# The last 128-column store as two halves of 64 rows on two queues, and the copy of x to the output in seven pieces instead of eight

## The chip, the cores and the metric

The kernel runs on one core of a Trainium2 chip, in one launch. Times are device microseconds of one execution of the program. Three runs of the kernel before took 177.51, 177.76 and 178.34 us; the median is 177.76 us. Beside them one execution was taken by the hardware profiler.

## The reference

What is computed, cut to what matters (`x` is 1 x 2048 x 512, bfloat16 in and out):

```python
xn = layernorm(x)                                   # over the 512 features, no weights
# A: a diagonal linear recurrence over the 2048 rows, with 512 complex states
Bu = einsum("bld,pd->blp", xn, B_bar)               # complex
h[t] = Lam_bar * h[t-1] + Bu[t]
a = 2 * einsum("blp,dp->bld", h, Cmat).real + xn * Dskip
# B: a gated feed-forward layer, F = 1376
b = (silu(xn @ w_gate) * (xn @ w_up)) @ w_down
return x + a + b
```

The output is thus the sum of x itself, a skip term, the recurrence and the feed-forward layer.

## The kernel before

The 2048 rows are 16 tiles of 128 rows; four tiles make a chunk of 512 rows. Each chunk goes through the normalization, the projection to the states (`bproj_chunk`, L384), the recurrence on VectorE (L394 to L426), the gate and up projections (`gateup_chunk`, L459) and the output (`out_chunk`). In the output stage every row tile has its sums collected in PSUM by TensorE: first the feed-forward part (`out_ffn`, L627), then the recurrence part (`out_ssm`, L640). The order on each engine is the order in which the kernel's Python code issues it (the schedule is manual); VectorE work is queued in a backlog and issued in portions between the matmuls.

The output reaches DRAM in two ways. For the first three chunks (rows 0 to 1535) x is copied to the output by DMA from DRAM to DRAM, without passing the on-chip memory (L896, L897): 1536 rows in eight pieces of 192 rows, all issued by SyncE (SP). Later GpSimd (POOL) issues DMAs that add to what stands there: the sums (L650) and the skip terms (L601). For the last chunk x and the skip term are already in `xall` on the chip; VectorE adds the PSUM tile to it (L643), and a plain store writes the finished rows (L647). SP issues the stores of the tiles 12, 13 and 14 as a whole, 128 rows of 512 columns.

The very last row tile, `n == NT - 1`, is cut into two column blocks (`out_blocks`, L606): columns 0 to 383, then 384 to 511. Block 0 is added by VectorE at L643 and stored by the queue of ScalarE (ACT), 128 rows of 384 columns. Meanwhile TensorE works on block 1, of which VectorE has x and the part already summed added beforehand (L646, into `rest`). The last add of the kernel is block 1 at L643; its store, 128 rows of 128 columns (32 KB, 256 bytes a row), is issued by SP at L647. In the profile, DMAs issued by SP are on queue q1, those of ACT on q10.

Each DMA of SP and ACT signals its landing on one of eight semaphores, handed out in turn in program order (DMAHW0 to DMAHW7); POOL's have eight others. At the end of the program (L941) SP waits for all of these semaphores one after the other, the hardware ones in the order 0 to 7, and then all engines meet in a barrier. In the kernel before, block 0 of the last tile signals DMAHW6 and block 1 DMAHW7.

Of the kernel before, what the change touches and what calls it, by code (L numbers as in the profile page):

```python
# [23 lines left out]
def kernel(  # L24
# [17 lines left out]
    nc = tc.nc  # L42
    _, L, D = A_x.shape
# [3 lines left out]
    CW = 512  # L47
    HW = CW // 2
    NT = L // 128
    NCH = L // CW  # L50
# [34 lines left out]
    out_v = out[0].rearrange("(n p) d -> p n d", p=128)  # L85
# [520 lines left out]
    def out_blocks(n):  # L606

        return ((0, 3 * D // 4), (3 * D // 4, D)) if n == NT - 1 else ((0, D),)
# [11 lines left out]
    def out_ffn(n, b=0):  # L620
        c, i = divmod(n, TPC)
        for lo, hi in out_blocks(n)[b:b + 1]:
            opened = c % 2 == 1 and b == 0
            if not opened:
                o_tiles[n, b] = bank((128, hi - lo))
            for fi in range(nfull):
                nc.tensor.matmul(o_tiles[n, b][:, 0:hi - lo], lhsT=gu(c, fi, fi + 1)[:, 0, i * 128:(i + 1) * 128],  # L627
                                 rhs=wd_sb[:, fi, lo:hi], start=(fi == 0 and not opened), stop=False)

    def out_ssm(n):  # L630
        c, i = divmod(n, TPC)
        last = n >= NT - TPC
        res = xall[:, n, :] if last else opool.tile([128, D], BF16, name="res")[:]
        for b, (lo, hi) in enumerate(out_blocks(n)):
            if b:
                out_ffn(n, b)
            o = o_tiles[n, b]
            for part in range(2):
                for q in range(NQ):
                    nc.tensor.matmul(o[:, 0:hi - lo], lhsT=w_tiles[c][:, part, q, i * 128:(i + 1) * 128],  # L640
                                     rhs=CF[:, part, q, lo:hi], start=False, stop=(part == 1 and q == NQ - 1))
            if last:
                V.tensor_tensor(out=res[:, lo:hi], in0=o[:, 0:hi - lo], in1=rest if b else res[:, lo:hi], op=ALU.add)  # L643
                if b == 0 and hi < D:
                    rest = jidx[:, 0:D - hi]
                    V.tensor_tensor(out=rest, in0=o[:, hi:D], in1=res[:, hi:D], op=ALU.add)  # L646
                (nc.sync if hi == D else nc.scalar).dma_start(out=out_v[:, n, lo:hi], in_=res[:, lo:hi])  # L647
            else:
                nc.scalar.copy(out=res[:, lo:hi], in_=o[:])  # L649
                nc.gpsimd.dma_start(out=out_v[:, n, lo:hi], in_=res[:, lo:hi], accum_op=ALU.add)  # L650
# [183 lines left out]
    def out_chunk(c):  # L834

        multiply(0)
        if c == 0:
            need("cf")
            load_rest()
        for n in range(c * TPC, (c + 1) * TPC):  # L840
            out_ffn(n)
            pump(nfull * 0.2163)
        if c % 2 == 0:
            out_rest(c)
            pump(2 * RT * 0.2163)
        need(f"ssm{c}")
        for n in range(c * TPC, (c + 1) * TPC):
            out_ssm(n)
            pump(2 * NQ * 0.2163)
# [9 lines left out]
    def queue_ssm(c):  # L859
        fwd, back = ssm_ops(c)  # L860
        queue(f"ssm{c}", fwd + back)
# [31 lines left out]
    nc.gpsimd.dma_start(out=dsk_bc[:], in_=A_Dskip.partition_broadcast(128))  # L893
    bproj_chunk(2)
    piece = (NCH - 1) * CW // 8
    for a in range(0, (NCH - 1) * CW, piece):  # L896
        nc.sync.dma_start(out=out[0, a:a + piece, :], in_=A_x[0, a:a + piece, :])  # L897
    queue_ssm(2)
    gateup_chunk(2)
    out_chunk(0)  # L900
# [45 lines left out]
```

## Time and profile before

| what | us |
|---|---|
| median of three runs (lowest, highest) | 177.76 (177.51, 178.34) |
| the profiled execution, its own time | 178.26 |
| its span, first to last instruction | 176.3 |
| TensorE busy with matmuls | 172.8 (98%) |
| VectorE, ScalarE, GpSimd busy | 158.9, 102.7, 27.1 |
| granted TensorE clock, share of full | 1.00 |

The span leaves out some 2 us of the execution that lie before the first or behind the last instruction. Times of single instructions below are counted from the span's start. "SPq" and "ACTq" are the issuing side of SyncE and ScalarE: the duration of a row is that of the issue, not of the transfer; "us to landing" runs from the issue's start until the whole transfer has signalled.

### The profile page before, as it was taken

The numbers are of one execution on the slowest core, as the hardware profiler recorded it, in microseconds if no ns is written. First come the engines' busy times: TensorE is split into PE (matmuls) and PEld (weight loads), VectorE is DVE, ScalarE is ACT, GpSimd is POOL, SyncE is SP. The second block draws the span as 40 slices with busy tenths as digits, with TensorE's granted clock in tenths as the row PEclk, the third lists the DMA queues.
The fourth block names the chain that finished last, engine by engine and source line by source line (L and its number), as shares of the span: only waits on it lengthen the run. The fifth ranks groups of instructions, "written<-read, shape, count | busy, mean of one in ns | idle before, by whom it ended". The sixth has DMA issues, their size and how long they took to land.

```text
span 176.3 us, 2456 instructions
## 1 busy us (share of the span) xinstructions
PE 172.8 (98%) x896; PEld 82.3 (47%) x896; DVE 158.9 (90%) x263; ACT 102.7 (58%) x186; POOL 27.1 (15%) x36
## 2 busy tenths in 40 slices
PE   8999999999999999999999999999999999999993
PEld 4444464454444464444444444445444444444542
DVE  2699999999999999899999999999999999689642
ACT  3159879895996689976044462014766662983100
POOL 5073210032000000000302500014100000530800
PEclk9999999999999999999999999999999999999999
DMA  5994979999999600220005830006410000597741
GB/s 169 366 343 63 168 148 209 283 185 307 110 203 264 170 4 0 55 57 0 2 0 109 91 42 0 0 4 67 52 22 0 2 4 0 70 174 113 81 102 60
DMA packets 34027, 18.05 MB, mean 102 GB/s; under 512 B 24512, under 2 KB 32832, under 8 KB 33888
## 3 DMA queue, kind: packets, MB, share of 16 engines
q1 hardware_dynamic: 30128, 14.26, 35.0%
q0 software_dynamic: 3456, 3.28, 14.9%
q10 hardware_dynamic: 432, 0.36, 0.6%
q8 instruction: 7, 0.11, 0.3%
q14 instruction: 4, 0.03, 0.1%
HBM read 8.33 MB, written 5.24 MB: 77 GB/s over the span
## 4 chain that ended last, share of the span: by engine, by line
PE 98%; DVE 0%; issue 0%
PE ps L459 29%; PE ps L627 20%; PE ps L640 16%; PE ps L384 16%; PE ps L503 8%; PE ps L552 3%; PE ps L801 2%; PE ps L700 2%; PE ps L617 2%; PE ps L239 1%; PE ps L244 0%; DVE xall L643 0%; PE ps L275 0%
## 5 line engine op out<-in xcount | busy, mean ns | idle before, releaser
L426 DVE TENSOR_TENSOR_SCAN g<-r_t,car,u 128x512 bf16<-128x512 f32 x24 | 28.8, 1262 | 0.0
L640 PE MATMUL ps<-CF,wt 128*128 128x512 bf16 (+2 forms) x136 | 28.5, 367 | 0.0
L384 PE MATMUL ps<-xnT,BT 128*128 128x512 bf16 x128 | 28.1, 379 | 0.0
L627 PE MATMUL ps<-wd_sb,guT 128*128 128x512 bf16 (+2 forms) x130 | 26.6, 363 | 0.0
L459 PE MATMUL ps<-xnT,wg 128*128 128x512 bf16 x96 | 24.6, 379 | 0.0
L459 PE MATMUL ps<-xnT,wu 128*128 128x512 bf16 x96 | 24.6, 379 | 0.0
L386 ACT CAST u<-ps 128x512 bf16<-128x512 f32 x32 | 18.0, 590 | 5.7 <-PE ps L384 5.2
L486 ACT CAST u<-ps 128x512 bf16<-128x512 f32 x30 | 18.0, 599 | 5.1 <-PE ps L459 5.1
L640 PEld LDWEIGHTS <-wt 128*128 128x128 bf16 x136 | 12.8, 98 | 15.1 <-DVE xall L597 0.4
L384 PEld LDWEIGHTS <-BT 128*128 128x128 bf16 x128 | 12.5, 98 | 14.9
L627 PEld LDWEIGHTS <-guT 128*128 128x128 bf16 x130 | 12.4, 98 | 13.9
L199 POOL TENSOR_TENSOR rstd<-ve,neg_half 128x1 f32<-128x1 f32 (+1 forms) x7 | 7.0, 1003 | 73.0 <-DVE ve L198 73.0
L649 ACT CAST res<-ps 128x512 bf16<-128x512 f32 x12 | 6.9, 583 | 18.6 <-PE ps L640 18.6
L589 ACT ACTIVATE xr<-xall,nb,rstd 128x512 bf16<-128x512 bf16 x16 | 11.8, 804 | 8.6 <-DVE xall L597 5.0
L650 POOL DMA_DIRECT2D out_dram<-res x12 | 10.5, 1042 | 36.0 <-ACT res L649 30.0
L459 PEld LDWEIGHTS <-wu 128*128 128x128 bf16 x96 | 9.4, 98 | 11.3
L485 ACT ACTIVATE guT<-ps 128x512 bf16<-128x512 f32 x20 | 12.0, 600 | 4.0 <-PE ps L459 3.6
L459 PEld LDWEIGHTS <-wg 128*128 128x128 bf16 x96 | 9.4, 98 | 10.6
L212 ACT ACTIVATE xn<-xall,nb,rstd 128x512 bf16<-128x512 bf16 x8 | 6.2, 816 | 8.2 <-DVE nb L202 8.2
L459 PE MATMUL ps<-xnT,w_end 128*128 128x512 bf16 x48 | 10.8, 379 | 0.0
L189 DVE BATCH_NORM_STATS2 stats<-xall 128x6 f32<-128x512 bf16 x16 | 10.8, 676 | 0.0
L394 DVE TENSOR_TENSOR pm<-g,c 128x2048 bf16<-128x2048 bf16 x8 | 9.8, 1221 | 0.1
(129 smaller groups left out, 237.8 us busy)
## 6 DMA issues: line engine op xcount, KB each, us to landing
out_dram<-in_A_x_dram SPq DMA_DIRECT2D x8, 192.0 KB, 3.2
out_dram<-res POOLq DMA_DIRECT2D x12, 128.0 KB, 3.1
out_dram<-xall POOLq DMA_DIRECT2D x3, 512.0 KB, 6.1
wd_sb<-in_B_w_down_dram SPq DMA_DIRECT2D x1, 1280.0 KB, 8.0
wu<-in_B_w_up_dram SPq DMA_DIRECT2D x4, 256.0 KB, 4.4
wg<-in_B_w_gate_dram SPq DMA_DIRECT2D x4, 256.0 KB, 5.1
xall<-in_A_x_dram SPq DMA_DIRECT2D x1, 1024.0 KB, 7.0
xall<-in_A_x_dram SPq DMA_DIRECT2D x1, 512.0 KB, 6.5
```

What stands on the lines that cost most here:

```text
L189: nc.vector.bn_stats(out=stats[:, n, 0, :], in_=xall[:, n, :])
L384: nc.tensor.matmul(ps[:] if c else by_k(ps[:]), lhsT=BT[:, part, k, q * 128:(q + 1) * 128], rhs=xnT[:, c, k, :] if c else xnT0[:, k], star ...
L386: nc.scalar.copy(out=u_tiles[c][:, part, q, :], in_=ps[:])
L426: V.tensor_tensor_scan(out=g()[:, part, q, :], data0=r_t[:, q:q + 1].to_broadcast([128, CW]), data1=u_tiles[c][:, part, q, :], initial=ini ...
L459: nc.tensor.matmul(ps[:fs, lo:hi], lhsT=wslice(groups, fi, k), rhs=xnT[:, c, k, lo:hi], start=(k == 0), stop=(k == KD - 1))
L485: nc.scalar.activation(out=gu(c, fi, fi + 1)[:fs, 0, :], in_=psg[:fs], func=ACT.Silu)
L486: nc.scalar.copy(out=u_pair[c][:fs, fi % 2, :], in_=psu[:fs])
L503: nc.tensor.matmul(ps[:, 0:(b - a) * 128], lhsT=tokens(i, k), rhs=groups[gi][:, k, 0:(b - a) * 128], start=(k == 0), stop=(k == KD - 1))
L589: nc.scalar.activation(out=box["xr"][:], in_=xall[:, n, :], func=ACT.Identity, scale=rstd[:, n:n + 1], bias=nb[:, n:n + 1])
L627: nc.tensor.matmul(o_tiles[n, b][:, 0:hi - lo], lhsT=gu(c, fi, fi + 1)[:, 0, i * 128:(i + 1) * 128], rhs=wd_sb[:, fi, lo:hi], start=(fi == ...
L640: nc.tensor.matmul(o[:, 0:hi - lo], lhsT=w_tiles[c][:, part, q, i * 128:(i + 1) * 128], rhs=CF[:, part, q, lo:hi], start=False, stop=(part ...
L650: nc.gpsimd.dma_start(out=out_v[:, n, lo:hi], in_=res[:, lo:hi], accum_op=ALU.add)
```

## The change

The store of block 1 of the last tile becomes two stores: rows 0 to 63 issued by SP, rows 64 to 127 issued by ACT. Both depend on the same last VectorE add. The store of block 0 stays on ACT, ahead of the new one. The copy of x keeps its 1536 rows, but in seven pieces: six of 192 rows and a last one of 384. So the number of DMAs that SP and ACT issue is the same as before.

```diff
@@ out_ssm
-                (nc.sync if hi == D else nc.scalar).dma_start(out=out_v[:, n, lo:hi], in_=res[:, lo:hi])
+                if b:
+                    for q, rows in ((nc.sync, slice(0, 64)), (nc.scalar, slice(64, 128))):
+                        q.dma_start(out=out_v[rows, n, lo:hi], in_=res[rows, lo:hi])
+                else:
+                    (nc.sync if hi == D else nc.scalar).dma_start(out=out_v[:, n, lo:hi], in_=res[:, lo:hi])
@@ the copy of x, between bproj_chunk(2) and queue_ssm(2)
     piece = (NCH - 1) * CW // 8
-    for a in range(0, (NCH - 1) * CW, piece):
-        nc.sync.dma_start(out=out[0, a:a + piece, :], in_=A_x[0, a:a + piece, :])
+    cuts = [*range(0, (NCH - 1) * CW - piece, piece), (NCH - 1) * CW]
+    for a, b in zip(cuts, cuts[1:]):
+        nc.sync.dma_start(out=out[0, a:b, :], in_=A_x[0, a:b, :])
```

In the built program the instruction order of TensorE, VectorE and GpSimd is the same as before. SP has one copy less. The three whole-tile stores of SP move by one semaphore, to DMAHW2, 3 and 4; block 0 of the last tile signals DMAHW5, ACT's half of block 1 DMAHW6 and SP's half DMAHW7.

## The prediction on record

> **What bounds the kernel now.** I first read the profile's page, for the share of each engine and of the chain that ended last:
>
> ```profile
> span 176.3 us, 2456 instructions
> PE 172.8 (98%) x896; PEld 82.3 (47%) x896; DVE 158.9 (90%) x263; ACT 102.7 (58%) x186; POOL 27.1 (15%) x36
> ...
> PE 98%; DVE 0%; issue 0%
> ```
>
> TensorE is the chain for 98% of the span. An edit that touches no matmul, and nothing a matmul waits for, can act only in what is left. So next the end: the chain of waits in order of time, its last pieces, and the timeline from 172.9 us on (start, duration, engine, line).
>
> ```profile
> 173.18 0.46 PE ps L640 x8
> 173.64 0.02 issue
> 173.67 0.29 DVE xall L643
> ```
>
> ```profile
> 173.25 0.35 ACTq L647 DMA_DIRECT2D out_dram<-xall  x1
> 173.67 0.29 DVE L643 TENSOR_TENSOR xall<-ps,jidx 128x128 bf16<-128x128 f32 x1 [0.25 <-PE ps L640]
> 173.98 0.33 SPq L647 DMA_DIRECT2D out_dram<-xall  x1
> ```
>
> The last matmul ends at 173.64, the last add at 173.96 (173.67 + 0.29), and SP issues the last store at 173.98. The span ends at 176.3: 2.3 us of tail in which no engine computes. What fills them? The DMA issues from 168 us on (size, landing time counted from the issue), and the instructions of the program's end in two windows, 174.3 to 175.0 and 175.4 to 176.4:
>
> ```profile
> out_dram<-xall SPq DMA_DIRECT2D x3, 128.0 KB, 1.7
> out_dram<-xall ACTq DMA_DIRECT2D x1, 96.0 KB, 1.6
> out_dram<-xall SPq DMA_DIRECT2D x1, 32.0 KB, 1.4
> ```
>
> ```profile
> L941 SPq EVENT_SEMAPHORE  x8: 28/28/28, 174.4 to 174.9; - x8
> ```
>
> ```profile
> L941 SPq EVENT_SEMAPHORE  x3: 17/17/28, 175.4 to 176.3; - x3
> ```
>
> The store lands 1.4 us after its issue, at 175.4. SP has by then passed eight of its closing waits, 0.07 us apart (0.5 us in seven steps), and sits in the ninth, the last store's; it passes at 175.4, and 0.9 us of barrier follow. So the tail is issue and landing 1.4, then 0.9 that the change leaves alone. Only the 1.4 can move.
>
> What it is made of, from windows of the DMA traffic (the last two columns are the busy share of the DMA engines and GB/s):
>
> ```profile
> 174.60:174.80 0.20, 0.00 (x0) 0.00 (x0) 0.00 (x0) 0.00 (x0) 0.00 (x0) 1.00 0.00 0
> 174.80:174.90 0.10, 0.00 (x0) 0.00 (x0) 0.00 (x0) 0.00 (x0) 0.00 (x0) 1.00 0.52 123
> 174.90:175.00 0.10, 0.00 (x0) 0.00 (x0) 0.00 (x0) 0.00 (x0) 0.00 (x0) 1.00 0.82 177
> 175.00:175.10 0.10, 0.00 (x0) 0.00 (x0) 0.00 (x0) 0.00 (x0) 0.00 (x0) 1.00 0.16 28
> 175.10:175.40 0.30, 0.00 (x0) 0.00 (x0) 0.00 (x0) 0.00 (x0) 0.00 (x0) 1.00 0.00 0
> ```
>
> 0.8 us pass before the first byte (0.33 of them the issue), the bytes take less than 0.3, and 0.3 pass until the signal. The movement, which a split could share out, is the smallest part.
>
> **The change part by part. The copy.** SP issues seven copies for eight:
>
> ```profile
> 52.76 5.45 SPq L897 DMA_DIRECT2D out_dram<-in_A_x_dram  x8
> 71.69 1.19 SPq L563 DMA_TRANSPOSE gu_more_rest<-g_last  x1
> ```
>
> ```profile
> L897 SPq DMA_DIRECT2D out_dram<-in_A_x_dram x8: 575/588/1027, 52.8 to 57.6; - x8
> ...
> DMA to landing us min/median/max: 2.7/3.2/3.7
> ```
>
> ```profile
> L650 POOL DMA_DIRECT2D out_dram<-res x12: 853/864/1892, 95.7 to 164.8; - x12
> ```
>
> One issue of 0.59 goes. Behind it SP has nothing to issue from 58.2 (52.76 + 5.45) to 71.69, where it waits for VectorE's product. The same bytes move; if the double piece took twice the longest landing, 7.4 us, it would be down by 66. The first to touch those rows is POOL's adding store at 95.7, 30 us later. I count 0. If the 13 us of cover were gone, the saved issue would be worth -0.59 and a late landing up to +3.7 to whoever waited.
>
> What the seven pieces do keep is the order of semaphores: ACT's half is waited for last but one at the end, SP's half last. With eight pieces SP's half would take the first of the eight, and seven more waits of 0.07 would follow its landing, +0.5. So I count 0 here, with that as the price of its absence.
>
> **The two issues.** SP's half starts where the whole store starts now. ACT is free: its issue for block 0 ends at 173.60 (173.25 + 0.35), 0.36 before the add that releases both halves. Behind the new wait ACT has nothing but the final barrier, and that stands behind SP's wait anyway. Issue durations by shape:
>
> ```profile
> L647 SPq DMA_DIRECT2D out_dram<-xall x4: 332/350/368, 168.6 to 174.0; - x4
> ...
> L647 ACTq DMA_DIRECT2D out_dram<-xall x1: 350/350/350, 173.2 to 173.2; - x1
> ```
>
> ```profile
> L161 SPq DMA_DIRECT2D CT<-in_B_w_down_dram x4: 417/424/527, 73.0 to 74.5; - x4
> ```
>
> 128 rows of 1024, 768 or 256 bytes cost 0.33 to 0.37, 32 rows in three strips 0.42: an issue does not shrink with its work in these rows. A 64-row issue is not in the trace; bounds 0.17 (by rows) and 0.42, I take 0.33, change 0.
>
> **The transfer.** Landing goes from 1.4 us at 32 KB to 1.7 at 128 KB: 0.3 for 96 KB, 0.003 per KB. The 16 KB taken off a half are worth 0.05, if the other half doesn't use the same DMA engines at that moment. I take -0.05, bounds -0.05 and 0.
>
> **The second queue at the same instant.** In the tail of before, no two hardware queues issue together. At the start they do: SP at 0.74 and ACT at 0.90 load 128 rows each (the timeline, then windows of the traffic, then the DMA queues' packets for 1.7 to 2.25 us).
>
> ```profile
> 0.74 0.40 SPq L128 DMA_DIRECT2D xall<-in_A_x_dram  x1
> ```
>
> ```profile
> 0.90 0.85 ACTq L131 DMA_DIRECT2D xall<-in_A_x_dram  x2
> ```
>
> ```profile
> 1.60:1.70 0.10, 0.10 (x2) 0.10 (x1) 0.00 (x0) 0.00 (x0) 0.00 (x0) 1.00 0.00 0
> 1.70:1.80 0.10, 0.10 (x2) 0.04 (x1) 0.00 (x0) 0.01 (x1) 0.02 (x1) 1.00 0.14 41
> ```
>
> ```profile
> DMA packets 70, 0.07 MB, mean 130 GB/s; under 512 B 0, under 2 KB 70, under 8 KB 70
> ...
> q1 hardware_dynamic: 70, 0.07, 79.0%
> ```
>
> SP's first packet starts by 1.80, 1.0 after its issue. Up to 2.25 all 70 packets are of q1: ACT's queue has moved nothing 1.35 us after its issue, though it issued only 0.16 behind SP. It is 0.45 behind SP, 0.3 more than the issues are apart. Alone, at 173.25, ACT's queue needs 0.9:
>
> ```profile
> 174.00:174.10 0.10, 0.00 (x0) 0.00 (x0) 0.00 (x0) 0.00 (x0) 0.00 (x0) 1.00 0.00 0
> 174.10:174.20 0.10, 0.00 (x0) 0.00 (x0) 0.00 (x0) 0.00 (x0) 0.00 (x0) 1.00 0.63 207
> ```
>
> So two queues that issue together seem to prepare their transfers partly one after the other. Bounds: 0 (they don't; the start is cold) and +0.5. Below nothing: if the 0.5 us between the end of an issue and the first byte goes by rows, halves that run side by side save 0.25. For 64 rows I take half of the 0.3 at the start, +0.15, as that is the only pair in the trace. The Trainium skill, "Perfetto Trace Analysis", section "DMA Instruction — HWDGE (DVE, Sync)", says that the descriptor generator is shared by the issuing engines and locked for one at a time, with the wait for the lock inside the profiled issue. By it the second half would be late by up to one issue, 0.33 as an estimate, and its issue row would be longer by that. The trace agrees only in part: the packets at the start come late, but no issue there shows such a wait.
>
> **The closing waits.** If ACT's half lands last, SP's own wait comes one step behind: +0.07. If SP's half lands last, 0. I take +0.07, as the row at the start has ACT behind.
>
> **Sum.** 0 + 0 - 0.05 + 0.15 + 0.07 = +0.17 us on the profiled execution's 178.26 (span 176.3 and 1.96 around it). That execution lies 0.50 above the median of the three runs, 177.76; applied to the median: 177.9 us, 0.1% more. A measurement of this kernel can tell about 0.5% (0.89 us) from no change, so this is no change.
>
> **Rivals.** (1) *The halves run side by side and each gets ready sooner.* For it: 0.5 us between issue and first byte isn't movement. Against: that gap is about the same for rows of 256 and 768 bytes, and the issue doesn't scale. -0.25 - 0.05 + 0.07 = -0.23: 177.5. (2) *Slower: one queue holds the other up in full.* Place: between the two issues and the first byte of the second half. Price: 0.45, as at the start, - 0.05 + 0.07: about +0.5, 178.2; it makes the kernel slower as soon as the hold exceeds the 0.05 saved. The worst row for it is ACT's second load, landed 3.4 us after its issue:
>
> ```profile
> xall<-in_A_x_dram ACTq DMA_DIRECT2D x1, 128.0 KB, 3.4
> ```
>
> Against ACT's 1.6 alone that is +1.8, 179.6; but at the start 256 KB loads crowd the same engines, in the tail nothing does. (3) *They share the DMA engines and nothing is gained:* movement as before, one more wait: +0.07, 177.8. The Trainium skill, "DMA: Bandwidth & Descriptors", section "Rules for kernel authors", speaks for this one: transfers of two partition halves serialize on the same sixteen engines, so one whole transfer is better. The trace before has no pair of half stores to test it.
>
> **How the numbers follow.** Forecast (+0.17) 0.40, side by side (-0.23) 0.15, full hold (+0.5) 0.20, shared engines (+0.07) 0.20; something in the rest of the span 0.05. All four named cases end within 0.5%; rival 2 passes +0.89 only near its worst row (0.04 of its 0.20). Faster by over 0.5%: 0.03, from the 0.05; slower: 0.04 + 0.02 = 0.06; within: 0.91. The range goes from rival 1 to rival 2 (177.5 to 178.2), widened by 0.2 on either side, as the runs of before lie 0.25 below and 0.58 above their median: 177.3 to 178.4.
>
> **What would show it.** In the profile after: matmuls unchanged up to 173.64; two half stores of 16 KB issued within 0.05 us of each other; ACT's landing later than SP's by about 0.15 to 0.2; nine closing waits of SP, the last released some 1.6 us after the add. Wrong would be: landings under 1.3 (rival 1), an issue of ACT near 0.7 or a landing over 1.8 (rival 2), equal landings at 1.4 (rival 3), or any stretch of TensorE before 173 that has moved.

## The result, and the profile after

Over 22 runs each, the changed kernel takes 178.46 us in the median (177.93 to 180.51) and the kernel before 177.84 (177.20 to 178.34). The ratio is 1.0039, with a 95% interval of 1.0024 to 1.0054: slower by 0.69 us (0.39% of 177.84), somewhere between 0.43 and 0.96. That is less than the 0.5% named in the prediction, yet the whole interval lies above 1, and the median lies just above the range's end of 178.4.

The profiled execution took 178.72 us with a span of 176.6 (before: 178.26 and 176.3). The two spans can't simply be subtracted, as the first view shows: the chain of waits of the changed kernel, last pieces.

```profile
172.77 0.46 PE ps L640 x8
173.23 0.02 issue
173.25 0.29 DVE xall L643
```

Before, the same pieces stood at 173.18, 173.64 and 173.67. TensorE is 0.41 us earlier here. Where does that come from? Two rows of TensorE's timeline at the start, of the kernel before and then of the changed one (start, duration):

```profile
6.54 0.61 PE L239 MATMUL ps<-ident,xall 128*128 128x128 bf16 x4
...
7.04 1.70 PE L503 MATMUL ps<-wu,CF 128*128 128x512 bf16 x7
```

```profile
6.35 0.39 PE L239 MATMUL ps<-ident,xall 128*128 128x128 bf16 x4
...
6.63 2.13 PE L503 MATMUL ps<-wu,CF 128*128 128x512 bf16 x9
```

The offset is there at 7 us (7.04 against 6.63), long before anything that the change touches, and it is the same 0.41 at the last matmuls (173.18 against 172.77). It is scatter of the start between executions (in the run below that has only the copy changed, the last matmuls begin at 172.12, earlier still); in between, the copy of x in seven pieces moved TensorE by nothing. So the stretch to compare is the tail, from the end of the last add to the end of the span: 173.96 to 176.34 before, 2.38 us; 173.54 to 176.56 after, 3.02 us. **The tail grew by 0.64 us**, which agrees with the 0.69 of the timed runs. I use the tail as the measure below; it leaves the start's scatter out.

What is in it? The timeline of the changed kernel behind its last add, and the issues of its two halves with the landing times (counted from the issue):

```profile
173.25 0.29 DVE L643 TENSOR_TENSOR xall<-ps,jidx 128x128 bf16<-128x128 f32 x1 [0.25 <-PE ps L640]
173.57 0.52 SPq L649 DMA_DIRECT2D out_dram<-xall  x1
173.58 0.56 ACTq L649 DMA_DIRECT2D out_dram<-xall  x1
```

```profile
out_dram<-xall SPq DMA_DIRECT2D x1, 16.0 KB, 1.7
out_dram<-xall ACTq DMA_DIRECT2D x1, 16.0 KB, 2.0
```

The halves are issued at the same instant, as the change wants it. But each issue takes 0.52 or 0.56 us where the whole store took 0.33, SP's half lands after 1.7 us where the whole store landed after 1.4, and ACT's half after 2.0. Windows of the DMA traffic (last column GB/s) show where the time lies:

```profile
174.60:174.70 0.10, 0.00 (x0) 0.00 (x0) 0.00 (x0) 0.00 (x0) 0.00 (x0) 1.00 0.00 0
174.70:174.80 0.10, 0.00 (x0) 0.00 (x0) 0.00 (x0) 0.00 (x0) 0.00 (x0) 1.00 0.20 49
174.80:174.90 0.10, 0.00 (x0) 0.00 (x0) 0.00 (x0) 0.00 (x0) 0.00 (x0) 1.00 0.48 95
174.90:175.00 0.10, 0.00 (x0) 0.00 (x0) 0.00 (x0) 0.00 (x0) 0.00 (x0) 1.00 0.11 21
175.00:175.10 0.10, 0.00 (x0) 0.00 (x0) 0.00 (x0) 0.00 (x0) 0.00 (x0) 1.00 0.39 82
175.10:175.20 0.10, 0.00 (x0) 0.00 (x0) 0.00 (x0) 0.00 (x0) 0.00 (x0) 1.00 0.41 77
```

There are two humps, one for each half: they don't move side by side. The view of the DMA queues from 174.50 to 175.01 (packets, MB, share of the engines' time) has one row, of SP's queue q1, so the first hump is SP's half alone:

```profile
q1 hardware_dynamic: 80, 0.02, 15.6%
```

And the first hump doesn't begin before 174.70, 1.1 us after its issue, where the whole store needed 0.8. SP's closing waits (two windows, 174 to 175 and 175.4 on) show the rest:

```profile
L946 SPq EVENT_SEMAPHORE  x7: 28/28/28, 174.1 to 174.5; - x7
```

```profile
L946 SPq EVENT_SEMAPHORE  x4: 17/22/28, 175.6 to 176.5; - x4
```

Seven of the nine pass early; the two of the halves pass at 175.6 and just after it, and the 0.9 us of barrier follow as before.

### The profile page after: what moved, and what is told of

It reads as the page before. It is cut to its first block, busy times and chain, and to the rows that moved or that the text cites. A ratio compares the mean times of both kernels' runs of the same rounds, so it can differ in the third digit from the quotient of the medians.

```text
span 176.6 us, 2441 instructions
## 1 busy us (share of the span) xinstructions
PE 171.6 (97%) x880; PEld 82.1 (46%) x896; DVE 158.8 (90%) x263; ACT 102.6 (58%) x186; POOL 27.1 (15%) x36
## 4 chain that ended last, share of the span: by engine, by line
PE 97%; issue 1%; ACT 0%; DVE 0%; ACTq 0%
PE ps L459 29%; PE ps L627 20%; PE ps L640 16%; PE ps L384 16%; PE ps L503 8%; PE ps L552 3%; PE ps L805 2%; PE ps L704 2%; PE ps L617 2%; PE ps L239 1%; ACT u L486 0%; PE ps L244 0%; DVE xall L643 0%; PE ps L275 0%; ACTq L486 0%
```

## The experiments

Ratios are against the kernel before, over the runs of both; a kernel without a ratio ran once, and its trace is read, not its time. Edits are against the changed kernel, except in the first experiment and in those with a table, where they are against the kernel before. The theories: **A**, two queues that issue at the same instant hold each other up; **B**, a store of 64 rows takes longer to prepare by itself, on any queue; **C**, the copy or the shifted semaphores cost the time. "Tail" is always the stretch from the end of the last add to the end of the span.

**Copy alone** (the last store whole again):

```diff
-    for a in range(0, (NCH - 1) * CW, piece):
+    cuts = [*range(0, (NCH - 1) * CW - piece, piece), (NCH - 1) * CW]
+    for a, b in zip(cuts, cuts[1:]):
```

> Only the copy of x is changed (seven pieces); the last store stays whole on SP. The tail, from the end of the last add to the end of the span, was 2.38 us before and 3.02 after. Theory A (two queues that issue at the same instant hold each other up) and theory B (a store of 64 rows takes longer to prepare by itself): the tail stays at 2.4 (the last store's semaphore is now the last but one, so 0.06 more is possible), ratio 1.000 within 0.002. Theory C (the copy or the shifted semaphores cost the time): the tail or the middle of the span grows, ratio near 1.004.

Ratio 1.0000 (0.9983 to 1.0017), tail 2.43. The copy costs nothing, in time or on the chain; C falls for it. The 0.05 in the tail are the one closing wait (0.06) that now stands behind the last store's.

**Split alone** (the copy in eight pieces again):

```diff
-    cuts = [*range(0, (NCH - 1) * CW - piece, piece), (NCH - 1) * CW]
-    for a, b in zip(cuts, cuts[1:]):
+    for a in range(0, (NCH - 1) * CW, piece):
```

> Only the split; the copy stays in eight pieces, so the SP half signals the first of the eight semaphores and the ACT half the last. Theories A and B: issues of 0.5 to 0.56 and landings of 1.7 and 2.0 as in the changed kernel, ratio 1.004 or a little more. The forecast's price for the lost order of the closing waits was +0.5; but if the SP half lands some 0.28 ahead of the ACT half, six waits of 0.06 behind it fit nearly into that gap, so that I now expect a tail of 3.05 to 3.15 against 3.02. Theory C: the tail goes back towards 2.4.

Ratio 1.0035 (1.0020 to 1.0051), tail 3.13, issues of 0.52 and 0.56 again. So the loss is the split's. The seven pieces are worth 0.11 in the tail (3.13 against 3.02), not the 0.5 that the prediction had as the price of their absence: SP's half, whose wait now stands first of the eight, lands at 174.94, and ACT's, whose wait is the last, at 175.20. Of the seven waits behind SP's half three begin ahead of ACT's landing, and these four behind it:

```profile
L945 SPq EVENT_SEMAPHORE  x4: 28/28/28, 175.2 to 175.4; - x4
```

The timed runs can't tell the 0.11: this ratio and the changed kernel's 1.0039 agree within their intervals.

**Both halves on SP**, so that no two queues issue together:

```diff
-                    for q, rows in ((nc.sync, slice(0, 64)), (nc.scalar, slice(64, 128))):
+                    for q, rows in ((nc.sync, slice(0, 64)), (nc.sync, slice(64, 128))):
```

> Both halves are issued by SP, one behind the other. Theory A: no two queues issue together, so each issue takes 0.33 to 0.37; the first half lands 1.4 after its issue, the second some 0.4 later; tail about 2.75, ratio about 1.002. Theory B (64 rows are slow by themselves): both issues take 0.52 and the first lands 1.7 after its issue; the second is 0.57 later; tail about 3.2, ratio 1.005.

Ratio 1.0054 (1.0034 to 1.0073), tail 3.34. The issues of the two halves (shortest, median, longest in ns, and starts):

```profile
L649 SPq DMA_DIRECT2D out_dram<-xall x2: 522/552/583, 173.7 to 174.2; - x2
```

Without any second queue the first issue still takes 0.52. A, as the main cause, falls. B has the first issue (0.52), the first landing (1.74) and the distance of the two issues (0.57) as expected; the second issue (0.58 for 0.52) and the tail (3.34 for 3.2) came out longer.

**One half alone:**

```diff
-                    for q, rows in ((nc.sync, slice(0, 64)), (nc.scalar, slice(64, 128))):
+                    for q, rows in ((nc.sync, slice(0, 64)),):
```

> Left out: the store of rows 64 to 127 of the last 128 columns; only SP's half is stored. Theory A: the issue takes 0.33, the landing 1.35 to 1.4 after it (16 KB less are worth 0.05), tail 2.35 to 2.45. Theory B: the issue takes 0.52 and the landing 1.7, tail 2.7.

```profile
L649 SPq DMA_DIRECT2D out_dram<-xall x1: 523/523/523, 173.5 to 173.5; - x1
...
DMA to landing us min/median/max: 1.7/1.7/1.7
```

This kernel leaves out the store of rows 64 to 127. Tail 2.76. Half the bytes, nothing beside them, and the store takes 0.19 longer to issue and 0.3 longer to land than the whole one. That is B, shown by itself.

**The halves cut by columns** (128 rows of 64 columns each):

```diff
-                    for q, rows in ((nc.sync, slice(0, 64)), (nc.scalar, slice(64, 128))):
-                        q.dma_start(out=out_v[rows, n, lo:hi], in_=res[rows, lo:hi])
+                    mid = (lo + hi) // 2
+                    for q, c0, c1 in ((nc.sync, lo, mid), (nc.scalar, mid, hi)):
+                        q.dma_start(out=out_v[:, n, c0:c1], in_=res[:, c0:c1])
```

> The last store is still two stores on two queues at the same instant, but cut by columns: 128 rows of 64 columns (16 KB) each. After the first four runs theory B stands (a store of 64 rows takes 0.52 to issue and 1.74 to land by itself; 128 rows take 0.33 and 1.44), and a part of theory A beside it (the second queue's half 0.27 later). Theory B: with 128 rows the issues are back at 0.33 and SP's half lands after 1.4; if the hold between the queues is a thing of its own, ACT's half lands after 1.7 and the tail is about 2.7, ratio 1.001 to 1.002; if the hold came from the slow preparation too, both land after 1.4 and the tail is 2.4 to 2.45, ratio 1.000. Theory A alone: issues of 0.52 and 0.56 and a tail of 3.0 as in the changed kernel.

```profile
L650 SPq DMA_DIRECT2D out_dram<-xall x1: 332/332/332, 173.0 to 173.0; - x1
L650 ACTq DMA_DIRECT2D out_dram<-xall x1: 367/367/367, 173.0 to 173.0; - x1
...
DMA to landing us min/median/max: 1.4/1.5/1.6
```

Ratio 1.0009 (0.9990 to 1.0027), tail 2.61. With 128 rows the slow issue is gone; SP's half lands after 1.4, as the whole store did with twice the bytes, and ACT's after 1.6. So a hold between the queues exists beside B, 0.16 in the trace (1.60 against 1.44, less than the landing after 1.7 that I had expected of a hold), and it leaves hardly a mark in the issue rows (0.37 against 0.33). Here the two halves do move side by side, as the queues' rows for 173.92 to 174.05 show:

```profile
q10 hardware_dynamic: 106, 0.01, 64.7%
q1 hardware_dynamic: 72, 0.01, 42.0%
```

**112 rows and 16 rows:** is every count of rows but 128 slow?

```diff
-                    for q, rows in ((nc.sync, slice(0, 64)), (nc.scalar, slice(64, 128))):
+                    for q, rows in ((nc.sync, slice(0, 112)), (nc.scalar, slice(112, 128))):
```

> Rows 0 to 111 on SP, rows 112 to 127 on ACT, at the same instant. Theory B1 (any count of rows other than 128 takes the slow way): both issues 0.5 or more, SP's landing 1.7 or later. Theory B2 (the preparation goes with the number of rows, fewer rows slower): SP's issue is near 0.35, ACT's at 0.6. Theory A (the hold goes with the partner's size): SP's half is hardly held, ACT's by more than 0.27.

```profile
L649 SPq DMA_DIRECT2D out_dram<-xall x1: 347/347/347, 173.1 to 173.1; - x1
L649 ACTq DMA_DIRECT2D out_dram<-xall x1: 380/380/380, 173.1 to 173.1; - x1
```

Neither is slow; tail 2.64. B1 and B2 both fall: 16 rows are as quick as 112. And ACT's 4 KB are held as long as its 16 KB were in the run before: they land 0.16 later than SP's half (1.62 against 1.46), so the hold doesn't grow with the partner's size either.

**Other shapes, read off the path.** In the next two kernels the last tile is stored as before, and the stores of the three tiles ahead of it (each with 1.7 us to itself) are cut in other ways, as a table in place of L647 (the line taken out isn't shown):

```diff
+                parts = {
+                    0: [(nc.sync, 0, 96, 0, D), (nc.sync, 96, 128, 0, D)],
+                    1: [(nc.sync, 0, 128, 0, 256), (nc.scalar, 0, 128, 256, D)],
+                    2: [(nc.sync, 0, 64, 0, D), (nc.sync, 64, 128, 0, D)],
+                }.get(n - (NT - TPC), [(nc.sync if hi == D else nc.scalar, 0, 128, lo, hi)])
+                for qu, r0, r1, c0, c1 in parts:
+                    qu.dma_start(out=out_v[r0:r1, n, c0:c1], in_=res[r0:r1, c0:c1])
```

> The last tile is stored as in the kernel before; the three tiles ahead of it, whose stores are off the path, are stored in other shapes, to read their issues: tile 12 as 96 and 32 rows, both on SP; tile 13 as two blocks of 128 rows and 256 columns, on SP and ACT at the same instant; tile 14 as 64 and 64 rows of 512 columns, both on SP. Theory B1 (every count other than 128 is slow): 96, 32 and 64 rows all take 0.5 or more, the 128-row blocks 0.33 to 0.37. Theory B2 (fewer rows, slower): 96 rows near 0.4, 64 rows 0.52, 32 rows near 0.6. Theory A: the pair of 128-row blocks takes 0.5 each. Tail unchanged at 2.4 in all of them.

The second kernel has 112 and 16 rows, 64 rows on SP beside 64 on ACT, and 128 rows twice with 256 columns.

> As the run before, with tile 12 as 112 and 16 rows on SP, tile 13 as two halves of 64 rows on SP and ACT at the same instant, tile 14 as two blocks of 128 rows and 256 columns on SP, one behind the other. Theory B1: 112 and 16 rows take 0.5 or more each; the halves of tile 13 take 0.52 and 0.56 as in the changed kernel, with rows of 1024 bytes as well; the two blocks of tile 14 take 0.33 to 0.37. Theory B2: 112 rows near 0.37, 16 rows over 0.6. Theory A: only the halves of tile 13 are slow.

From the first of them, the window of tile 12 (96 rows, then 32) and that of tile 14 (64, then 64):

```profile
L653 SPq DMA_DIRECT2D out_dram<-xall x2: 350/385/420, 168.5 to 168.9; - x2
```

```profile
L653 SPq DMA_DIRECT2D out_dram<-xall x2: 523/553/583, 172.0 to 172.6; - x2
```

From the second, tile 12 (112, then 16) and tile 14 (128 and 128):

```profile
L653 SPq DMA_DIRECT2D out_dram<-xall x2: 349/386/422, 168.1 to 168.5; - x2
```

```profile
L653 SPq DMA_DIRECT2D out_dram<-xall x2: 363/394/424, 171.6 to 172.0; - x2
```

In each of these pairs the second issue takes 0.06 or 0.07 more than the first. Apart from that, 16, 32, 96, 112 and 128 rows all cost about 0.35, and 64 rows 0.52, with 512 columns as with 128. The pair of 64-row halves on two queues takes 0.52 and 0.56 as in the changed kernel. The pair of 128-row blocks on two queues (tile 13 of the first kernel) takes 0.36 and 0.37, and again ACT's lands 0.16 later than SP's (1.89 against 1.73).

What I expected of the tails, 2.4, was wrong: they are 2.76 and 2.74, though the last store itself was nearly as before (landings of 1.50 and 1.48 against 1.45). With three more DMAs its semaphore falls in the middle of the closing order, and the five waits behind it are paid in full. In the second kernel they stand in a row with its own, after the landing:

```profile
L947 SPq EVENT_SEMAPHORE  x6: 28/28/28, 175.0 to 175.3; - x6
```

Six waits, from the first to the last 0.3 us: 0.06 a step.

**48 and 80 rows.** Is it the number 64, or counts in the middle?

```diff
-                    for q, rows in ((nc.sync, slice(0, 64)), (nc.scalar, slice(64, 128))):
+                    for q, rows in ((nc.sync, slice(0, 48)), (nc.scalar, slice(48, 128))):
```

> The last store as 48 rows on SP and 80 rows on ACT at the same instant, the copy in seven pieces as in the changed kernel. After eight runs 64 rows took 0.52 to issue wherever they stood, but 16, 32, 96, 112 and 128 rows 0.33 to 0.42. Theory D (the number 64 alone is slow, not the cut by rows): both issues 0.33 to 0.38, landings of 1.45 on SP and 1.6 on ACT, tail 2.6, ratio 1.001. Theory E (counts in the middle, between 32 and 96, are slow): both issues near 0.5, tail near 3.0, ratio 1.004.

```profile
L649 SPq DMA_DIRECT2D out_dram<-xall x1: 345/345/345, 172.7 to 172.7; - x1
L649 ACTq DMA_DIRECT2D out_dram<-xall x1: 377/377/377, 172.8 to 172.8; - x1
...
DMA to landing us min/median/max: 1.4/1.5/1.6
```

Ratio 1.0006 (0.9991 to 1.0022), tail 2.57. The same split over two queues, by rows, with other numbers of rows, costs 0.19 in the tail and nothing that the timed runs can tell. D stands: of the cuts by rows, only the one with 64 is slow.

**More shapes,** with the same table as above:

```diff
+                    0: [(nc.sync, 0, 48, 0, D), (nc.sync, 48, 128, 0, D)],
+                    1: [(nc.sync, 32, 96, 0, D), (nc.sync, 0, 32, 0, D), (nc.sync, 96, 128, 0, D)],
+                    2: [(nc.sync, 0, 80, 0, D), (nc.sync, 80, 128, 0, D)],
```

> The last tile as in the kernel before; ahead of it on SP alone: tile 12 as 48 then 80 rows, tile 13 as the middle rows 32 to 95 and then 32 and 32, tile 14 as 80 then 48. Theory D: only the 64 middle rows take 0.52; 48 and 80 take 0.35 as the first of a tile and 0.42 as the second. Theory E: 48 and 80 take nearly 0.5 as well. If the place of the rows mattered (a half that begins at row 0 or 64), the middle 64 rows would take 0.35.

The windows of tiles 12 and 13:

```profile
L653 SPq DMA_DIRECT2D out_dram<-xall x2: 352/382/411, 167.6 to 168.0; - x2
```

```profile
L653 SPq DMA_DIRECT2D out_dram<-xall x3: 407/567/569, 169.4 to 170.6; - x3
```

48 and 80 rows are quick. The 64 rows from 32 to 95 take 0.57 (I had expected 0.52), so it isn't the place of the rows. What I had not expected: the 32 rows issued right behind them take 0.57 as well, and only the second 32 are back at 0.41. So in this run the issue behind a 64-row store is slow too; no other run has such an issue with other than 64 rows.

**Small ones first,** with the same table:

```diff
+                    0: [(nc.sync, 0, 32, 0, D), (nc.sync, 32, 128, 0, D)],
+                    1: [(nc.sync, 0, 16, 0, D), (nc.sync, 16, 128, 0, D)],
+                    2: [(nc.sync, 0, 60, 0, D), (nc.sync, 60, 128, 0, D)],
```

> As the run before: tile 12 as 32 then 96 rows, tile 13 as 16 then 112 rows, tile 14 as 60 then 68 rows, all on SP. Theory D: the first ones take 0.33 to 0.37 with 32, 16 and 60 rows alike, the second ones 0.42, and no issue of this run reaches 0.5. Theory E: 60 and 68 rows take near 0.5. Counts that 16 doesn't divide (60, 68) may run on fewer DMA engines and land later; their issue is what is read.

No issue reaches 0.5; 32 and 16 rows as the first of a tile take 0.35 and 0.31, and tile 14's are 0.38 for 60 rows and 0.26 for 68, the one second issue that is shorter than the first:

```profile
L653 SPq DMA_DIRECT2D out_dram<-xall x2: 256/319/382, 171.2 to 171.6; - x2
```

None of the versions was measured faster than the kernel before: with every cut over two queues the later half lands later than the whole store did (1.55 with 48 and 80 rows, against 1.45).

## Why the prediction was wrong

The landings can be taken apart further. The table has, from the traces' packets, the time from the issue's start to the first packet, from there to the end of the last packet, and from there to the signal:

| store | to the first packet | moving | to the signal | landing |
|---|---|---|---|---|
| whole, 128 rows of 256 bytes (before) | 0.83 | 0.27 | 0.35 | 1.45 |
| 64 rows, alone | 1.18 | 0.23 | 0.34 | 1.75 |
| 64 rows, SP's half (the changed kernel) | 1.18 | 0.23 | 0.34 | 1.74 |
| 64 rows, ACT's half (the changed kernel) | 1.44 | 0.23 | 0.35 | 2.02 |
| 128 rows of 128 bytes, SP's half | 0.83 | 0.23 | 0.38 | 1.44 |
| 128 rows of 128 bytes, ACT's half | 0.90 | 0.23 | 0.46 | 1.60 |

By the prediction's own steps:

- **What bounds the kernel** held. TensorE's stream is the same from 7 us on, only the tail moved, and in it only the time from issue to landing and the closing waits.
- **The copy at 0** held (ratio 1.0000 alone). Its side effect on the closing order has the right sign, but 0.11 in place of 0.5: the prediction left out that the waits behind SP's half can pass while ACT's half is on its way.
- **The two issues** is the step that failed. It took 0.33 for a 64-row issue, "change 0", with bounds of 0.17 and 0.42 from shapes of 128 and 32 rows, as if the cost had to lie between or go with the count. It is 0.52, outside both bounds, and SP's half lands 0.30 later for it (1.74 against 1.45), alone as well as in the pair: its first packet comes 0.34 later (1.175 against 0.831), its movement is 0.04 shorter.
- **The transfer at -0.05** held as movement: 0.23 in place of 0.27. But no landing of the column halves shows it (1.44 against 1.45), because the signal took longer there; SP's 48 rows landed 0.06 sooner (1.39).
- **The second queue at +0.15** came near in size where no issue was slow: ACT's half landed 0.16 behind SP's in the column halves, with 48 and 80 rows, and with 112 and 16. That is luck in part. The 0.15 was half of the 0.3 at the start of the kernel, and no row gave the half; and its mechanism, a later start of the second transfer, makes only 0.04 to 0.11 of the 0.16 in these cuts: 0.07 in the column halves, where the other 0.08 come behind the last packet. (Of the 0.07, 0.03 may be ACT's own: block 0, issued by ACT alone, needed 0.86 to its first packet.) With 64-row halves it is 0.27, nearly all of it ahead of the first packet, so there the term was 0.12 short.
- **The closing wait at +0.07** held: 0.06.

The terms as measured: 0.30 for the shape (with the shorter movement in it), 0.27 for the second queue, 0.06 for the wait, 0.63 of the 0.64 that the tail grew. With 48 and 80 rows the same split grows the tail by 0.19, against the forecast of 0.17, so what took the time out of the range is what the 64 rows cost: 0.30 in the first half and 0.12 more between the halves, neither of which the forecast had.

Of the rivals, the full hold (+0.5) came nearest in time, but its mechanism isn't what happened: the first half was late with no partner at all. The side-by-side gain occurred in no run; the earliest half, 48 rows, landed after 1.39 against 1.45.

The Trainium skill's rule in "DMA: Bandwidth & Descriptors", section "Rules for kernel authors", is that two partition halves serialize and that one whole transfer is to be used instead. The two humps of the 64-row halves agree with it, and so does the ratio of 1.0006 for 48 and 80 rows, where nothing is gained. The lock that the Trainium skill, "Perfetto Trace Analysis", section "DMA Instruction — HWDGE (DVE, Sync)", describes has its wait inside the issue row. No issue row of a second half on ACT shows such a wait: ACT's issue was only 0.03 or 0.04 longer than SP's, both among the column halves (0.37 against 0.33) and in the changed kernel (0.56 against 0.52), while its landing came 0.16 and 0.27 later.

What stays open: why 64 rows, and of the counts tried (16, 32, 48, 60, 64, 68, 80, 96, 112, 128) only they, take the longer issue, and what the second half waits for. The longer issue was seen on stores from SP and ACT, at three places in the tile and with 256 and 1024 bytes a row; loads of 64 rows were not tried.

## What to carry to other kernels

The small transfer that ends this kernel spent 1.18 of its 1.45 us ahead of its first packet and behind its last, and 0.27 on movement: cutting it in two equal halves saved some 0.04 of movement, and it added a second half that landed 0.16 or more behind the first, and another closing wait. Look for that share before you split a last store. Don't interpolate a DMA's issue cost between shapes of the trace; put the new shape on a store that is off the path, and read its row. And when the start of a kernel scatters, compare the tail from the last common instruction, not the spans.

## What the runs showed that was not expected

A store of 64 rows takes 0.52 to 0.58 us to issue and about 0.3 us longer to land, where 48 rows take 0.35 and 80 rows 0.37; in one run the issue of 32 rows behind it on the same queue took 0.57, where others took 0.41. Two queues that issue together can move their packets side by side, and the second one's signal still came 0.16 later. The order in which the program's end waits for its semaphores is worth 0.06 us a place: the same last store gave tails of 2.38, 2.43 and 2.74 us with none, one and five waits behind its own.
